# Attention and a Fourier filter layer on one core: loads of k and v as 96 x 6 rows, a shared filter fold, and a reordered last batch

## The chip, the cores and the metric

The kernel runs on one core of one Trainium2 chip. Times are device microseconds of one execution. The number to predict is the median over such executions, which for the kernel before is 233.95 us. TensorE (PE in the profile) does matmuls, VectorE (DVE) and ScalarE (ACT) elementwise work, GpSimd (POOL) elementwise work and the loads that change the type, SyncE (SP) issues other DMAs.

## The reference

There are 8 batches, 8 heads, 576 positions, 64 elements per head; the model width is 512.

```python
def _attn_ref(q, k, v, g_norm):
    kv = np.einsum('bhsd,bhse->bhde', k, v)
    out = np.einsum('bhsd,bhde->bhse', q, kv)
    rms = np.sqrt(np.mean(out * out, axis=-1, keepdims=True) + 1e-06)
    return out / rms * g_norm

def _moe_ref(x, w_proj, filter_fft, w_out):          # x: heads side by side, (8, 576, 512)
    proj = x @ w_proj
    x1, x2, x3 = ...                                 # thirds of proj
    X2 = np.fft.rfft(x2, axis=1)
    H = np.fft.rfft(filter_fft, axis=0)[None]
    x2_conv = np.fft.irfft(X2 * H, axis=1)
    y = x1 * x2_conv * x3
    return y @ w_out
```

## The kernel before, in words

All matmuls are in bf16. `load_kv` and `load_q` bring k, v and q of a batch to SBUF through GpSimd's DMA queue, which turns fp32 into bf16 on the way. k and v lie as 128 partitions by 4 rows of the sequence, which covers 512 of 576 rows; the other 64 rows are a load of their own (`kvt`, L75). Buffers are double: batch b uses set b % 2. All loads of the start (q, k, v of batch 0, three parts of `w_proj`, the filter twice, q, k, v of batch 1, `w_out`) are on that one queue in this order. The filter comes once straight (`fa`, three rows to a partition, L150) and once mirrored through an indirect DMA with an index tile (`fc`, L153); both load 112 rows (NL) of which 97 are used.

For a batch, `kv` (L247) multiplies k by v in five chunks of the sequence and copies the 64 x 64 blocks into a block-diagonal tile `kvblk`; `qtr` transposes q; `att_o` multiplies the two, squares the result on ScalarE (L298) and scales it by g_norm on VectorE or ScalarE (L300 to L303); `att_r` sums the squares over a head with a matmul and takes the reciprocal root on ScalarE; `att_x` multiplies to x, and `fold` (VectorE) builds sums and differences of x over thirds and mirror images, so that the Fourier transform of length 576 becomes matmuls of 97 and 128 rows. `proj2` projects the folded x to x2, `fft(b, g)` transforms it in three groups g (two VectorE products per group for the complex product with the filter's spectrum HH, their sum on Pool at L426 or on VectorE at L428; group 2 is one product with HM, L433) into Y. `proj13` makes x1 (ScalarE copy) and the gate g13 = x1 * x3 (VectorE, L450); `inv` is the inverse transform with its unfolding on VectorE, and `outp` multiplies by `w_out` and stores.

The filter's own spectrum is made once: `filter_angles` and `filter_tables` compute its sines and cosines FH on VectorE and ScalarE, `tables` transposes the inverse's tables IV on TensorE and copies them to FW and FX on VectorE, `fold_filter` (L347) adds and subtracts `fa` and `fc` into `ff` (two VectorE operations), `gen_h(g)` multiplies FH by ff (L364, L368), and ScalarE scales the result to HH and HM.

The main program is L609 to L698. Ahead of the loop, TensorE gets filler matmuls (`warm`), then batch 0's attention in two halves (two head pairs each). Each pass of the loop over b runs the filter layer of batch b interleaved with the attention of batch b + 1 and the output of batch b - 1. Pass b = 0 has an order of its own that holds the filter's spectrum. The last batch ends in `last` (L537): an inverse split so that the first and last row blocks are done first, then the output of batch 6 and five pieces of output (`out1`).

The program is written in this order, but a scheduler orders each engine's instructions by when it believes their inputs to be ready, with program order as the priority, and inserts the waits. `tc.keep_in_program_order(ins)` pins an instruction behind everything written before it for its engine. PSUM is one pool of four tiles (`psp`), each two banks; a matmul group waits for a free one. GpSimd's and SyncE's DMAs have a limited number in flight: a further one waits for an older one to land.

Of the kernel before, what the change touches and what calls it, by code (L numbers as in the profile page):

```python
# [15 lines left out]
P = 128  # L16
# [4 lines left out]
def kernel(  # L21
# [39 lines left out]

    NR = S // 64
    kvm = [[consts.tile([P, H, 4, D], BF16, name="%sm%d" % (n, i)) for n in "kv"] for i in range(2)]
# [3 lines left out]
    def load_kv(b, *parts):  # L67
        for h0, h1 in parts:
            for i, src in enumerate((k, v)):
                nc.gpsimd.dma_start(  # L70
                    out=kvm[b % 2][i][:, h0:h1].rearrange("p h c d -> p h (c d)"),
                    in_=bass.AP(tensor=src.tensor, offset=src.offset + (b * H + h0) * S * D,
                                ap=[[4 * D, P], [S * D, h1 - h0], [1, 4 * D]]))
                if h0 == 0:
                    nc.gpsimd.dma_start(out=kvt[b % 2][i][:TAIL], in_=src[b, :, 4 * P:S, :].transpose([1, 0, 2]))  # L75
# [73 lines left out]
    NL = 112  # L149
# [70 lines left out]
    FX = consts.tile([P, 4, P], BF16)  # L220

    def tables():
        nc.vector.memset(FX[0:96, 0], 0.0)
        d0, d1 = (psp.tile([P, 2, 8, P], BF16, name="ps_ft", tag="ps")[:, 0] for _ in range(2))
        lo, hi = slice(0, 64), slice(64, P)
        tr, cp = nc.tensor.transpose, nc.vector.tensor_copy
        for i in range(2, 6):
            tr(d0[:, i], IV[:, i, 0:P], ident)
        tr(d0[0:96, 0], IV[:, 0, 0:96], ident)
        tr(d0[96:P, 6], IV[:, 1, 0:32], ident)  # L230
        for r in (lo, hi):
            tr(d0[r, 7], IV[:, 1, 32:96], ident)
        for i in range(2, 6):
            tr(d1[lo, i], IV[:, i, P:SB], ident)
        for i in (3, 5):
            tr(d1[hi, 6 + i // 5], IV[:, i, P:SB], ident)
        cp(out=FW[:, 0, 2:6], in_=d0[:, 2:6])
        cp(out=FW[lo, 1, 2:6], in_=d1[lo, 2:6])
        cp(out=FX[hi, 2:4], in_=d1[hi, 6:8])
        cp(out=FW[0:96, 0, 0], in_=d0[0:96, 0])  # L240
        cp(out=FX[96:P, 0], in_=d0[96:P, 6])
        cp(out=FX[:, 1], in_=d0[:, 7])
# [4 lines left out]
    def kv(b, j0=0, j1=NDC):  # L247
        (km, vm), (kt, vt) = kvm[b % 2], kvt[b % 2]
        kvp = ps_tile("ps_kv")
        for j in range(j0, j1):  # L250
            for c in range(NSC):
                for hp in range(2):
                    h = 2 * j + hp
                    kk, vv = (km[:, h, c], vm[:, h, c]) if c < 4 else (kt[:, h], vt[:, h])
                    mm = nc.tensor.matmul(kvp[64 * hp:64 * hp + 64, 0, j * D:(j + 1) * D], kk, vv,  # L255
                                          start=(c == 0), stop=(c == NSC - 1))
                    if b == 1:
                        tc.keep_in_program_order(mm)
        for h in range(2):
            r = slice(64 * h, 64 * h + 64)  # L260
            o_ = kvblk[b % 2][r, j0:j1, r]
            i_ = kvp[r, 0, j0 * D:j1 * D].rearrange("p (j e) -> p j e", e=D)
            if b == 0 and j0 == 0:
                nc.vector.tensor_copy(out=o_, in_=i_)
            else:
                nc.scalar.copy(out=o_, in_=i_)  # L266
# [23 lines left out]
    def att_o(b, j):  # L290
# [9 lines left out]
        if b == 0 or b == 1 and j != 2:  # L300
            nc.vector.tensor_scalar_mul(out=o_, in0=op[:, :, 0:TH], scalar1=g_col)
        else:
            nc.scalar.activation(out=o_, in_=op[:, :, 0:TH], func=AF.Copy, scale=g_col)  # L303
# [43 lines left out]
    def fold_filter():  # L347
        ff = hst['ff'] = work.tile([P, 2, 3, DM], BF16, name="ff", tag="ff")
        for i, op in enumerate((nc.vector.tensor_add, nc.vector.tensor_sub)):
            tc.keep_in_program_order(op(out=ff[:N1, i], in0=fa[:N1], in1=fc[:N1]))  # L350
# [52 lines left out]
    def fft(b, g):  # L403
# [7 lines left out]
        if g < 2:  # L411
# [13 lines left out]
            if g or b in (0, B - 1):  # L425
# [111 lines left out]
    def last(b):  # L537
# [21 lines left out]
        proj13(b, NDC - 1)  # L559
# [30 lines left out]
        for c in (0, 2):  # L590
            outp(b - 1, c)
# [21 lines left out]
    for jj in range(2):  # L613
# [8 lines left out]
        fold(0, jj)  # L622
    filter_tables()
    tables()
    for b in range(B):
# [7 lines left out]
        if b == 0:  # L633
# [6 lines left out]
            gen_h(2)  # L640
            qtr(1, (0,))
            fft(0, 0)
            qtr(1, (1,))
            fft(0, 2)
            kv(1)
# [8 lines left out]
        if b == 0:  # L654
# [3 lines left out]
            att_r(1, 1)  # L658
            proj13(0, 2)
            att_x(1, 0)  # L660
            fold(1, 0)
            att_o(1, 2)
# [7 lines left out]
        for dc in range(NDC if nxt else NDC - 1) if b else ():  # L670
            if dc < 3:
                add = (fft(b, (1, 0, 2)[dc]) if dc or not nxt else None) or (dc and add)
            if nxt and dc == 0:
# [3 lines left out]
            else:  # L677
                if nxt:
                    att_o(b + 1, dc)
# [3 lines left out]
            if nxt:  # L683
                att_r(b + 1, dc)
                if dc % 2:
                    att_x(b + 1, dc // 2)
                    fold(b + 1, dc // 2)
            if b and nxt and dc in (1,):
                outp(b - 1, 2 * (1,).index(dc))
        if not nxt:  # L690
            last(b)
# [37 lines left out]
```

## Time and profile before

| what | us |
|---|---|
| median of 14 runs | 233.95 |
| lowest and highest | 232.27 and 235.31 |
| the profiled execution, its own time | 234.17 |
| its span, first to last instruction | 232.1 |
| TensorE busy | 210.2 |
| VectorE busy | 193.7 |
| ScalarE busy | 157.8 |
| Pool busy | 73.0 |
| mean granted TensorE clock | 0.986 |

All times within the profile count from the start of the span. In a line of the timeline the first number is the start, the second the busy time of the group; then come engine, line, operation, output <- inputs, shape and count, and in brackets how long the engine stood idle before and what released it. In the chain of work the two numbers are start and duration. The row by slices cuts the span into 40 parts of 5.8 us; a digit is the busy share in tenths. Releasers are inferred from semaphores, so a named one can be the last of several.

### The profile page before, as it was taken

Reading aid. Unit: us, or ns where it says so; the run is one execution under the profiler, and the core shown is the slowest. Engines: PE = TensorE matmul, PEld = TensorE weight load, DVE = VectorE, ACT = ScalarE, POOL = GpSimd, SP = SyncE. Lnnn points to the kernel's source line nnn. Section 1 sums busy time; section 2 is a strip of 40 time slices with the busy share of each in tenths; the row PEclk is TensorE's granted clock in tenths of the full one; section 3 lists DMA queues with packets and bytes.
Section 4 is the critical chain, followed back from the end, with each engine's and each line's share of the span. In section 5 each row is a group of like instructions: output and inputs, shape, how many; then the busy total and the mean of one; then the engine's idle time right before and its main releaser. Section 6 shows DMA issues by size and latency. Waiting matters only on the chain.

```text
span 232.1 us, 4858 instructions
## 1 busy us (share of the span) xinstructions
PE 210.2 (91%) x1941; PEld 128.4 (55%) x1967; DVE 193.7 (83%) x369; ACT 157.8 (68%) x230; POOL 73.0 (31%) x87
## 2 busy tenths in 40 slices
PE   4967789779999999999999999999999999999970
PEld 1434265464657565755766576656675666566520
DVE  6967776898997998798897989797979897997940
ACT  2738946875869597958975897769776977533340
POOL 7983363960650056003800380004000300016010
PEclk9979999999999999999999999999999999999997
DMA  5999999999897349932991299150033003500086
GB/s 63 149 174 227 240 192 199 190 191 189 97 187 133 93 45 183 172 80 67 174 214 25 71 162 205 34 134 1 12 82 90 3 0 93 136 0 3 0 214 193
DMA packets 45543, 27.37 MB, mean 118 GB/s; under 512 B 22242, under 2 KB 40674, under 8 KB 45522
## 3 DMA queue, kind: packets, MB, share of 16 engines
q0 software_dynamic: 40240, 17.90, 60.4%
q1 hardware_dynamic: 5042, 8.78, 14.4%
q10 hardware_dynamic: 240, 0.39, 0.6%
q8 instruction: 15, 0.25, 0.4%
q14 instruction: 6, 0.05, 0.1%
HBM read 33.88 MB, written 9.44 MB: 187 GB/s over the span
## 4 chain that ended last, share of the span: by engine, by line
PE 75%; POOL 8%; DMA 6%; DVE 3%; issue 3%; ACT 2%; POOLq 0%; DVEq 0%
PE ps_x L444 23%; PE ps_out L506 10%; DMA fc<-in_moe_filter_fft_dram,fidx 6%; PE ps_x L393 5%; PE ps_qT L279 3%; PE ps_o L297 3%; PE ps_r L312 3%; PE ps_x L384 3%; PE ps_x L399 3%; PE ps_invo L470 2%; POOL Y L426 2%; PE ps_kv L255 2%; PE ps_inve L470 2%; PE ps_x L387 2%; PE ps_out L528 2%
## 5 line engine op out<-in xcount | busy, mean ns | idle before, releaser
L444 PE MATMUL ps_x<-x,wp 128*128 128x288 bf16 x512 | 69.0, 286 | 0.0
L444 PEld LDWEIGHTS <-wp 128*128 128x128 bf16 x512 | 49.2, 98 | 14.3 <-issue 0.9
L426 POOL TENSOR_TENSOR Y<-tpw 128x1024 bf16<-128x1024 f32 (+1 forms) x10 | 23.5, 2353 | 70.3 <-DVE tpw L424 70.3
L450 DVE TENSOR_TENSOR g<-ps_x,x 128x576 bf16<-128x576 f32 x32 | 24.0, 753 | 10.9 <-ACT x L448 7.5
L70 POOL DMA_DIRECT2D km<-in_k_dram x9 | 8.0, 885 | 61.7 <-PE ps_kv L255 58.2
L313 ACT ACTIVATE rstd<-ps_r,bias_eps 128x576 bf16<-128x576 f32 x32 | 23.3, 743 | 5.5 <-PE ps_r L312 5.5
L506 PE MATMUL ps_out<-wo,yg 128*128 128x512 bf16 x99 | 25.6, 379 | 0.7
L448 ACT CAST x<-ps_x 128x576 bf16<-128x576 f32 x32 | 20.5, 641 | 8.1 <-PE ps_x L444 8.1
L514 ACT COPY ot<-ps_out 128x1024 f32<-128x1024 f32 (+1 forms) x17 | 15.9, 937 | 14.6 <-PE ps_out L506 14.6
L298 ACT ACTIVATE sq<-ps_o 128x576 bf16<-128x576 f32 x32 | 20.5, 650 | 6.3 <-PE ps_o L297 5.6
L423 DVE TENSOR_TENSOR tpw<-ps_X,HH 128x1024 f32<-128x1024 f32 (+1 forms) x16 | 19.5, 1222 | 3.4 <-PE ps_X L421 1.7
L424 DVE TENSOR_TENSOR tpw<-ps_X,HH 128x1024 f32<-128x1024 f32 (+1 forms) x16 | 19.4, 1213 | 0.0
L303 ACT ACTIVATE osb<-ps_o,g_col 128x576 bf16<-128x576 f32 x25 | 18.5, 739 | 0.0
L393 PE MATMUL ps_x<-wp,ab 128*128 128x512 bf16 x61 | 15.5, 381 | 1.6 <-DVE ab L339 1.3
L506 PEld LDWEIGHTS <-yg 128*128 128x128 bf16 x112 | 11.0, 98 | 10.8
L474 ACT COPY os<-ps_invo 128x576 f32<-128x576 f32 x14 | 9.0, 640 | 10.5 <-PE ps_x L387 5.1
L288 ACT COPY qT<-ps_qT 128x1152 bf16<-128x1152 bf16 x14 | 15.6, 1119 | 0.7
L297 PE MATMUL ps_o<-qT,kvblk 128*128 128x288 bf16 x64 | 13.0, 297 | 2.7 <-ACT kvblk L266 1.5
L312 PE MATMUL ps_r<-sq,ind 128*128 128x288 bf16 x64 | 13.4, 295 | 2.2 <-ACT sq L298 1.8
L606 PE MATMUL ps_w<-kvblk,ind 128*128 128x512 bf16 x31 | 10.3, 481 | 3.9 <-DVE ind L103 3.4
L321 DVE TENSOR_TENSOR x<-osb,rstd 128x1152 bf16<-128x1152 bf16 x16 | 12.1, 754 | 1.7 <-ACT rstd L313 1.7
L79 POOL DMA_DIRECT2D qb<-in_q_dram x16 | 12.6, 791 | 1.4 <-POOLq L713 0.8
(210 smaller groups left out, 405.7 us busy)
## 6 DMA issues: line engine op xcount, KB each, us to landing
out_dram<-ot SPq DMA_DIRECT2D x28, 256.0 KB, 3.3
qb<-in_q_dram POOLq DMA_DIRECT2D x16, 288.0 KB, 6.4
km<-in_k_dram POOLq DMA_DIRECT2D x7, 512.0 KB, 6.4
vm<-in_v_dram POOLq DMA_DIRECT2D x7, 512.0 KB, 8.1
wp<-in_moe_w_proj_dram POOLq DMA_DIRECT2D x3, 512.0 KB, 12.0
out_dram<-ot SPq DMA_DIRECT2D x6, 128.0 KB, 3.3
fa<-in_moe_filter_fft_dram POOLq DMA_DIRECT2D x1, 672.0 KB, 15.4
km<-in_k_dram POOLq DMA_DIRECT2D x2, 256.0 KB, 4.2
```

The costliest lines, as they stand in the source:

```text
L297: nc.tensor.matmul(op[:, h, 0:TH], kvblk[b % 2][:, j], s['qT'][:, 2 * (j % 2) + j // 2, h * TH:(h + 1) * TH], start=True, stop=True)
L298: nc.scalar.activation(out=s['sq'][:, j].rearrange("p (a b) -> p a b", a=2), in_=op[:, :, 0:TH], func=AF.Square)
L312: nc.tensor.matmul(r2[:, h, 0:TH], ind, s['sq'][:, j, h * TH:(h + 1) * TH], start=True, stop=True)
L313: nc.scalar.activation(out=s['rstd'][:, j].rearrange("p (a b) -> p a b", a=2), in_=r2[:, :, 0:TH], func=AF.Abs_reciprocal_sqrt, scale=1.0 ...
L393: nc.tensor.matmul(pp[:, h], ab[:, j, h * SB:h * SB + P], wp[:, j, DM:2 * DM], start=(j == 0), stop=(j == NDC - 1))
L423: nc.vector.tensor_mul(out=t_[:n, 0], in0=xp[:n], in1=HH[:n, g, 1:3])
L424: nc.vector.tensor_mul(out=t_[:n, 1], in0=xp[:n], in1=HH[:n, g, 0:2])
L426: nc.gpsimd.tensor_add(out=Y[:n, 2 * g:2 * g + 2], in0=t_[:n, :, 0], in1=t_[:n, :, 1])
L444: nc.tensor.matmul(pp[:, h, 0:TH], w_, x[:, j, h * TH:(h + 1) * TH], start=(j == 0), stop=(j == NDC - 1))
L448: nc.scalar.copy(out=x1, in_=pp[:, :, 0:TH])
L450: nc.vector.tensor_mul(out=st[b]['g13'][:, dc].rearrange("p (a b) -> p a b", a=2), in0=pp[:, :, 0:TH], in1=st[b]['x1', dc])
L506: nc.tensor.matmul(pp[:, cc], yg[:, dc, c * P:(c + 1) * P], wo[:, dc], start=(dc == 0), stop=(dc == NDC - 1))
```

## The change

- k and v of batches 0 and 1 are loaded as 96 partitions by 6 rows, which covers all 576 rows, so their tail loads are gone. Their `kv` runs six chunks of 96 rows in place of five. Later batches are as before, in wider tiles.
- The filter is loaded 96 rows at a time; the 97th, one row of 512, comes through SyncE's queue into each of `fa` and `fc`.
- `fold_filter` becomes six operations: Pool takes the third of the three filter rows of each partition (both the sum and the difference), VectorE the other two, all pinned.
- `tables` comes ahead of `filter_tables`, its copies are pinned, and a clearing of FX moves to the start. The first copy into `kvblk` of batch 0 moves from VectorE to ScalarE, as does the scale of batch 0's last head pair.
- In pass 0, kv(1) comes ahead of gen_h(2) and fft(0, 2); att_x(1, 0) and att_o(1, 2) come ahead of proj13(0, 2).
- In the last batch, both remaining transforms come ahead of proj13(7, 1); of group 0's sum Pool makes half and VectorE the other; half the output of batch 6 comes ahead of the inverse, and proj13(7, 2) behind the inverse's matmuls.

```diff
@@ -59,19 +59,21 @@
 
 
 
     NR = S // 64
-    kvm = [[consts.tile([P, H, 4, D], BF16, name="%sm%d" % (n, i)) for n in "kv"] for i in range(2)]
+    kvm = [[consts.tile([P, H, 6, D], BF16, name="%sm%d" % (n, i)) for n in "kv"] for i in range(2)]
     kvt = [[consts.tile([P, H, D], BF16, name="%st%d" % (n, i)) for n in "kv"] for i in range(2)]
     qb = [consts.tile([P, 4, NR * D], BF16, name="qb%d" % i) for i in range(2)]
 
     def load_kv(b, *parts):
+        n, C = (96, 6) if b < 2 else (P, 4)
         for h0, h1 in parts:
             for i, src in enumerate((k, v)):
                 nc.gpsimd.dma_start(
-                    out=kvm[b % 2][i][:, h0:h1].rearrange("p h c d -> p h (c d)"),
+                    out=kvm[b % 2][i][:n, h0:h1, 0:C].rearrange("p h c d -> p h (c d)"),
                     in_=bass.AP(tensor=src.tensor, offset=src.offset + (b * H + h0) * S * D,
-                                ap=[[4 * D, P], [S * D, h1 - h0], [1, 4 * D]]))
-                if h0 == 0:
+                                ap=[[C * D, n], [S * D, h1 - h0], [1, C * D]]))
+                if h0 == 0 and b > 1:
                     nc.gpsimd.dma_start(out=kvt[b % 2][i][:TAIL], in_=src[b, :, 4 * P:S, :].transpose([1, 0, 2]))
 
     def load_q(b):
@@ -146,7 +148,9 @@
     nc.gpsimd.iota(fidx, pattern=[[-1, 3]], base=S, channel_multiplier=-3)
     nc.gpsimd.memset(fidx[0:1, 0:1], 0)
 
-    NL = 112
+    NL = N1 - 1
+    for t in (fa, fc):
+        nc.sync.dma_start(out=t[NL:N1, 0], in_=moe_filter_fft[TH:TH + 1])
     nc.gpsimd.dma_start(out=fa[:NL], in_=bass.AP(
         tensor=moe_filter_fft.tensor, offset=moe_filter_fft.offset, ap=[[3 * DM, NL], [1, 3 * DM]]))
     for a in range(3):
@@ -218,12 +222,12 @@
 
     FW = consts.tile([P, 2, 6, P], BF16)
     FX = consts.tile([P, 4, P], BF16)
+    nc.vector.memset(FX[0:96, 0], 0.0)
 
     def tables():
-        nc.vector.memset(FX[0:96, 0], 0.0)
         d0, d1 = (psp.tile([P, 2, 8, P], BF16, name="ps_ft", tag="ps")[:, 0] for _ in range(2))
         lo, hi = slice(0, 64), slice(64, P)
-        tr, cp = nc.tensor.transpose, nc.vector.tensor_copy
+        tr, cp = nc.tensor.transpose, lambda **kw: tc.keep_in_program_order(nc.vector.tensor_copy(**kw))
         for i in range(2, 6):
             tr(d0[:, i], IV[:, i, 0:P], ident)
         tr(d0[0:96, 0], IV[:, 0, 0:96], ident)
@@ -248,22 +252,20 @@
         (km, vm), (kt, vt) = kvm[b % 2], kvt[b % 2]
         kvp = ps_tile("ps_kv")
         for j in range(j0, j1):
-            for c in range(NSC):
+            n, nc_ = (96, 6) if b < 2 else (P, NSC)
+            for c in range(nc_):
                 for hp in range(2):
                     h = 2 * j + hp
-                    kk, vv = (km[:, h, c], vm[:, h, c]) if c < 4 else (kt[:, h], vt[:, h])
+                    kk, vv = (km[:n, h, c], vm[:n, h, c]) if b < 2 or c < 4 else (kt[:, h], vt[:, h])
                     mm = nc.tensor.matmul(kvp[64 * hp:64 * hp + 64, 0, j * D:(j + 1) * D], kk, vv,
-                                          start=(c == 0), stop=(c == NSC - 1))
+                                          start=(c == 0), stop=(c == nc_ - 1))
                     if b == 1:
                         tc.keep_in_program_order(mm)
         for h in range(2):
             r = slice(64 * h, 64 * h + 64)
             o_ = kvblk[b % 2][r, j0:j1, r]
             i_ = kvp[r, 0, j0 * D:j1 * D].rearrange("p (j e) -> p j e", e=D)
-            if b == 0 and j0 == 0:
-                nc.vector.tensor_copy(out=o_, in_=i_)
-            else:
-                nc.scalar.copy(out=o_, in_=i_)
+            nc.scalar.copy(out=o_, in_=i_)
 
     def qtr(b, jjs=(0, 1)):
 
@@ -297,7 +299,7 @@
             nc.tensor.matmul(op[:, h, 0:TH], kvblk[b % 2][:, j], s['qT'][:, 2 * (j % 2) + j // 2, h * TH:(h + 1) * TH], start=True, stop=True)
         nc.scalar.activation(out=s['sq'][:, j].rearrange("p (a b) -> p a b", a=2), in_=op[:, :, 0:TH], func=AF.Square)
         o_ = s['o'][:, j].rearrange("p (a b) -> p a b", a=2)
-        if b == 0 or b == 1 and j != 2:
+        if b == 0 and j < 3 or b == 1 and j != 2:
             nc.vector.tensor_scalar_mul(out=o_, in0=op[:, :, 0:TH], scalar1=g_col)
         else:
             nc.scalar.activation(out=o_, in_=op[:, :, 0:TH], func=AF.Copy, scale=g_col)
@@ -346,8 +348,9 @@
 
     def fold_filter():
         ff = hst['ff'] = work.tile([P, 2, 3, DM], BF16, name="ff", tag="ff")
-        for i, op in enumerate((nc.vector.tensor_add, nc.vector.tensor_sub)):
-            tc.keep_in_program_order(op(out=ff[:N1, i], in0=fa[:N1], in1=fc[:N1]))
+        for eng, n, s_ in ((nc.gpsimd, N1 - 1, slice(2, 3)), (nc.vector, N1, slice(0, 1)), (nc.vector, N1 - 1, slice(1, 2))):
+            for i, op in enumerate((eng.tensor_add, eng.tensor_sub)):
+                tc.keep_in_program_order(op(out=ff[:n, i, s_], in0=fa[:n, s_], in1=fc[:n, s_]))
 
     def gen_h(g):
 
@@ -422,7 +425,10 @@
             t_ = work.tile([P, 2, 2, DM], FP32, name="tpw", tag="tpw", bufs=2)
             nc.vector.tensor_mul(out=t_[:n, 0], in0=xp[:n], in1=HH[:n, g, 1:3])
             nc.vector.tensor_mul(out=t_[:n, 1], in0=xp[:n], in1=HH[:n, g, 0:2])
-            if g or b in (0, B - 1):
+            if g == 0 and b == B - 1:
+                nc.gpsimd.tensor_add(out=Y[:n, 1], in0=t_[:n, 1, 0], in1=t_[:n, 1, 1])
+                return lambda: nc.vector.tensor_add(out=Y[:n, 0], in0=t_[:n, 0, 0], in1=t_[:n, 0, 1])
+            if g or b == 0:
                 nc.gpsimd.tensor_add(out=Y[:n, 2 * g:2 * g + 2], in0=t_[:n, :, 0], in1=t_[:n, :, 1])
                 return
             return lambda: nc.vector.tensor_add(out=Y[:n, 2 * g:2 * g + 2], in0=t_[:n, :, 0], in1=t_[:n, :, 1])
@@ -556,7 +562,8 @@
                 for g in (1, 2):
                     nc.tensor.matmul(pb[:, h, dc * 64:(dc + 1) * 64], Y[:, 2 * g + h, dc * P:(dc + 1) * P],
                                      IV[:, 2 * g + h, P:SB], start=(g == 1), stop=(g == 2))
-        proj13(b, NDC - 1)
+        for dc in (2, 3):
+            proj13(b, dc)
         osa = work.tile([P, 2, 2 * M], FP32, name="osa", tag="tpw", bufs=2)
         osb_ = work.tile([P, NDC * 64], FP32, name="osb_", tag="os")
         nc.scalar.copy(out=osa, in_=tiles[1][:, :, 0:2 * M])
@@ -587,8 +594,7 @@
         dv.tensor_add(out=w[:, :, 64:S].rearrange("p j (x c) -> p j x c", c=2 * P)[:, :, :, 64:P], in0=ub, in1=rr_)
         mid = slice(P, 7 * 64)
         dv.tensor_mul(out=yg[:, :, mid], in0=w[:, :, mid], in1=g13[:, :, mid])
-        for c in (0, 2):
-            outp(b - 1, c)
+        outp(b - 1, 2)
         act, dve = nc.scalar.copy, nc.vector.tensor_copy
         q0, q1, q2 = nc.sync, nc.scalar, nc.gpsimd
         ot = lambda tag, bufs: work.tile([P, 4, DM] if tag == "tpw" else [P, 2, DM] if tag == "ot" else [P, 3, DM],
@@ -620,8 +626,8 @@
         warm(3)
         att_x(0, jj)
         fold(0, jj)
+    tables()
     filter_tables()
-    tables()
     for b in range(B):
         nxt = b + 1 < B
         proj2(b)
@@ -637,12 +643,12 @@
             gen_h(1)
             gen_h(0)
             fft(0, 1)
-            gen_h(2)
             qtr(1, (0,))
             fft(0, 0)
             qtr(1, (1,))
+            kv(1)
+            gen_h(2)
             fft(0, 2)
-            kv(1)
         elif nxt:
             kv(b + 1)
             qtr(b + 1, (0,))
@@ -656,10 +662,10 @@
             att_o(1, 1)
             att_r(1, 0)
             att_r(1, 1)
+            att_x(1, 0)
+            att_o(1, 2)
             proj13(0, 2)
-            att_x(1, 0)
             fold(1, 0)
-            att_o(1, 2)
             att_o(1, 3)
             att_r(1, 2)
             att_r(1, 3)
@@ -667,27 +673,32 @@
             fold(1, 1)
             proj13(0, 3)
             fins = [inv(0, (0, 1))]
-        for dc in range(NDC if nxt else NDC - 1) if b else ():
+        for dc in range(NDC) if b and nxt else ():
             if dc < 3:
-                add = (fft(b, (1, 0, 2)[dc]) if dc or not nxt else None) or (dc and add)
-            if nxt and dc == 0:
+                add = (fft(b, (1, 0, 2)[dc]) if dc else None) or (dc and add)
+            if dc == 0:
                 proj13(b, 0, (0,))
                 att_o(b + 1, 0)
                 proj13(b, 0, (2,))
             else:
-                if nxt:
-                    att_o(b + 1, dc)
+                att_o(b + 1, dc)
                 proj13(b, dc)
             if dc == 2 and add:
                 add()
-            if nxt:
-                att_r(b + 1, dc)
-                if dc % 2:
-                    att_x(b + 1, dc // 2)
-                    fold(b + 1, dc // 2)
-            if b and nxt and dc in (1,):
-                outp(b - 1, 2 * (1,).index(dc))
+            att_r(b + 1, dc)
+            if dc % 2:
+                att_x(b + 1, dc // 2)
+                fold(b + 1, dc // 2)
+            if dc == 1:
+                outp(b - 1, 0)
         if not nxt:
+            for dc, g in enumerate((1, 0)):
+                add = fft(b, g)
+                if dc:
+                    fft(b, 2)
+                    add()
+                proj13(b, dc)
+            outp(b - 1, 0)
             last(b)
             continue
         if b:
```

## The prediction

> **What bounds the kernel now.** I read the page first. TensorE is busy for 91% of the span, and the row by slices shows where it isn't: slices 1 to 9 (one is 5.8 us) and the last.
>
> ```profile
> PE 210.2 (91%) x1941; PEld 128.4 (55%) x1967; DVE 193.7 (83%) x369; ACT 157.8 (68%) x230; POOL 73.0 (31%) x87
> ...
> PE   4967789779999999999999999999999999999970
> ```
>
> From 54 us to 212 us TensorE hardly stops, and the change leaves those batches alone. What it touches is the first 54 us, where TensorE waits, and the last 20. So I next read the chain of work that ended last, between 16 and 34 us:
>
> ```profile
> 16.55 13.68 DMA fc<-in_moe_filter_fft_dram,fidx
> 30.23 0.03 issue
> 30.25 0.05 DVEq L350
> 30.30 0.04 issue
> 30.35 0.92 DVE ff L350
> 31.27 0.75 issue
> 32.02 1.76 DVE ff L350
> 33.79 0.05 issue
> 33.83 2.78 PE ps_h L364 x12
> ```
>
> The gathered filter `fc` lands at 30.23 us, VectorE folds for 3.4 us, then TensorE starts the spectrum `ps_h`. One chain is not a bound, so I asked the timeline what TensorE and VectorE did meanwhile (start, busy us, engine, line):
>
> ```profile
> 12.34 0.32 PE L255 MATMUL ps_kv<-vm,km 128*64 128x64 bf16 x8 [0.62 <-DMA vm<-in_v_dram]
> ...
> 23.11 0.42 DVE L237 COPY FW<-ps_ft 128x512 bf16<-128x512 bf16 x1 [0.61 <-PE ps_ft L232]
> 23.45 0.75 DVE L321 TENSOR_TENSOR x<-osb,rstd 128x1152 bf16<-128x1152 bf16 x1
> ...
> 33.83 0.39 PE L364 MATMUL ps_h<-ff,FH 97*128 97x512 bf16 x1 [0.66 <-DVE ff L350]
> ```
>
> TensorE waited only 0.66 us for the fold: a second chain (k, v of batch 0, attention, `x`, fold of `x`, proj2, proj13) is just behind. Landing the filter sooner alone is worth 0.66 us; both chains must move. The second has a stall of its own: `x` at 23.45, although its `rstd` was done at 22.22, because a table copy (L237) stood before it on VectorE, waiting for TensorE.
>
> At the end I read the timeline and SyncE's waits:
>
> ```profile
> 213.13 0.22 PE L553 MATMUL ps_invo<-IV,Y 97*128 97x96 bf16 x1 [0.40 <-POOL Y L426]
> ...
> 222.04 0.57 PEld L531 LDWEIGHTS <-yg 128*64 128x64 bf16 x8 [0.53 <-DVE yg L589]
> ...
> 228.68 0.47 SPq L534 DMA_DIRECT2D out_dram<-ot__3310  x1
> ```
> ```profile
> SPq L534 <- DMA out_dram<-ot__3288: 0.9, 1, 0.9
> ```
>
> The last result is in SBUF at 225.73 us (L532), but its second half is issued at 228.68, after an earlier store has landed. The stretches from 221 to 230 us show a DMA share of 0.68 to 1.07: the end is a queue of stores.
>
> **What the Trainium skill says.** "DMA: Bandwidth & Descriptors", section "Why a DMA increments its semaphore by 16 and not by 1": a load of 96 partitions spreads over 16 engines, an odd count over few. That speaks for 96 rows plus a single row; no run here shows 97. The same page, "Specifications", asks for at least 512 B per transfer. The trace agrees in part: the tail of k in batch 0 (128 B writes, 131 KB read) took 1.36 us between landings (9.14 to 10.5), in batch 1 only 0.45. "GPSIMD Engine Reference", section 3.1: a two-input op is about twice as slow as on VectorE. The trace agrees: L426 on Pool 2.36 us, the same add on VectorE (L428) 1.21. Its section 1 says that Pool's SBUF interface is shared with VectorE instructions of two SBUF inputs; the trace has no such pair that tells a price.
>
> **Part 1, the loads.** A landing is the issue plus the time to landing. q of batch 0 is in at 7.7, its k and v at 16.05: 8.35 us for 2.36 MB. 1.96 of that are the two tails; the four halves (0.524 MB read) took 1.45 to 1.7. With 96 x 6 rows the tails are gone and a part reads 0.590 MB. At the slowest of the halves (1.7) it would take 1.9, at batch 1's rate (1.05 MB in 2.5 us) 1.4; I take 1.55, so 6.2 instead of 8.35: 2.15 sooner (0.75 to 2.75; a loss is excluded, fewer packets with the same bytes). The filter took from 24.9 (last `wp` landing) to 30.23; 96 of 112 rows save a seventh of 5.33 us, 0.76. `fc` then lands at 27.3. Two row loads go to SyncE's queue, which holds only `g_col` then: nothing. Pool issues two fewer DMAs per batch at 0.7 us, which are ahead of `wp`; issue is not what bounds, since the queue is some 5 us deep by then.
>
> **Part 2, the chain of x.** The warm-up matmuls end at 11.72, so kv can start at 11.75 instead of 12.34 and, without the wait for the tail at 12.77, ends at 12.45 with its 24 matmuls (20 before). The copy on ScalarE, idle here, costs 0.63 from kv to `ps_o` (18.62 to 19.25 in the second half) against 1.22 now: `ps_o` at 13.1, not 14.37. From there to the end of `rstd` it is 3.88 us now at a TensorE clock of 0.50 to 0.69 (14 to 18 us), 2.97 in the second half at full clock; I take a mean gain, 1.6 for the second kv. `rstd` of the second half then ends at 20.7 instead of 22.22; the scale of head pair 3, moved to ScalarE (0.73, ahead of `rstd`), makes it 21.45. `x` starts there, not at 23.45, as the table copies are pinned behind the fold; `x` and fold take 2.6 instead of 2.95 (one copy less): 24.1 against 26.40. From the fold's end TensorE needs 6.7 us for proj2, proj13(0,0) and (0,1) (26.46 to 33.16), whose weights land before 23. So `ps_h` starts at 30.85 instead of 33.83: **3.0 sooner**. The copies now lie after the fold: 1.8 us, to 25.9, beside proj2; its third PSUM tile needs them at 25.8. That is the cover, and it is thin: 0.1 to 0.3 if it fails.
>
> **The filter's fold.** VectorE now does two thirds: a 97x1536 op is 1.755, so about 0.62 for 512, four make 2.5; Pool two of 512 at half of 2.36, 2.4. From 27.3 both end at 29.8, 1.0 before TensorE is ready. If they take turns at SBUF the sum is 4.9: 32.2, so 1.4 of the gain lost. I take no cost and keep that end. Pool's two ops stand in its queue; behind them are the loads of batch 2, which have 8 us to spare.
>
> **Part 3, batch 1's attention.** kv(1) goes before gen_h(2), so `ps_o` no longer waits 0.85 for the copy on ScalarE and gen_h(2) fills that gap; 8 matmuls more cost 0.16 (40 take 0.78). VectorE is nearly full from 37.4 to 53.15 with about 1.7 idle, of which an earlier att_o(1,2) can win a part. From both sides: +0.3 to -1.2; I take **-0.4**. k and v of batch 1 land at 27.3 + 2.8 (q) + 2 x 2.75 = 35.6; kv(1), pinned, is due at 36.8: 1.2 to spare.
>
> **Part 4, the end.** TensorE's work is only reordered. Of Pool's 2.36 us add, half moves to VectorE (0.7), and the 0.40 and 0.04 that TensorE waits at 213 go. But proj13(7,2) behind the inverse puts its gate multiply (0.75) into VectorE's last row of work, full from 214.84 to 221.99; this starts 0.65 sooner (inverse at 212.0, no stop). So L531 is where it was, 222.05: zero, -0.4 to +0.7. Stores: 0.52 MB (outp(6,0)) leave the queue of 2.36 MB for a time when DMA is idle (212 to 220). At the 240 GB/s of 222 to 228 us that is 2.2 us of transfer; since the last stores wait also for their results and issue, I take half: **-1.1**, 0 to -2.2.
>
> **Sum:** -3.0 - 0.4 - 1.1 = -4.5. The profiled execution took 234.17 us (span 232.1, 2.07 around it), 0.22 over the median of 233.95. So 229.45, say 229.5.
>
> **Rivals.**
> - *Bytes bind, not packets.* For: batch 1's tails took only 0.45. Then only the filter's seventh is gained: `fc` at 29.5, folded at 32.0, `ps_h` at 32.1 (-1.7); with -0.3 and -0.5 for the rest that is -2.5: 231.4. The same time comes out if Pool and VectorE take turns. Against: 8.35 us in batch 0.
> - *All of it, at full clock.* If the shorter idle time before 14 us keeps the clock up, x gains 0.5 more; with -1.2 in batch 1 and -1.8 at the end: -6.5, 227.4.
> - *Pool becomes the bound of the fold* (the slower side). Before, Pool issued batch 2's loads between 30.75 and 37.2, ahead of work that the program has before them, and each waited for an older load to land (vt for km: 1.6). If the fold is ordered behind all these, its last issue waits for batch 1's k (32.9), so Pool folds from 33.7 to 36.1, and `ps_h` starts at 36.2: +2.4, less the end's 1.1: +1.3, 235.2. It decides for slower once Pool's fold ends after about 35.6. Against: its ops are pinned behind wo's load and come first in the program.
> - *It nets to nothing:* the fold half as late, or kv(1) waiting, with no gain at the end: 233.7.
>
> **Numbers.** Forecast 0.56 (228.3 to 230.7 of its own), bytes bind 0.16, full gain 0.12, Pool 0.10, nothing 0.06. 0.3%, 0.7 us, is about what a measurement here can tell from no change. Faster 0.84, same 0.06, slower 0.10. The range takes in the two faster rivals with most of their width, 226.8 to 232.4, and leaves out Pool and nothing.
>
> **What would show it.** `fc` landing near 27.3 (if 29.5, bytes bind); ps_kv from 11.75; `x` of the second half before 22; `ps_h` from 30.9, waiting for proj13 rather than `ff`; Pool's `ff` between 27 and 30, ahead of batch 2's km (behind it, the slower rival); ps_o of batch 1 8.6 after `ps_h` (9.0 now); no wait for Pool at the last inverse; L531 at the same distance from batch 7's start; the last store issued within 2 us of L532's last copy (2.95 now). The forecast is wrong if TensorE waits anew before 54 us, on kv(1) or on PSUM.

## The result, and the profile after

| | before | after |
|---|---|---|
| median, us | 233.94 (47 runs, 232.27 to 235.59) | 231.14 (10 runs, 230.24 to 232.39) |
| profiled execution: time, span | 234.17, 232.1 | 231.05, 229.3 |
| TensorE, VectorE busy in it | 210.2, 193.7 | 209.6, 194.8 |

The ratio after to before is 0.9884, with a 95% interval of 0.9864 to 0.9903: 2.8 us faster, where 4.5 was forecast. The sign and the range held, and the end went as described. The start gained much less than forecast, and one of its steps, the filter's fold at no cost, failed. The forecast's own range (228.3 to 230.7) was missed by 0.4, and the time is nearer the 231.4 of the rival "bytes bind". That it is not further off is in part luck: the end gave more than forecast, where the start gave less.

The page of after shows the start less empty, and the end in one slice:

```profile
PE 209.6 (91%) x1956; PEld 128.0 (56%) x1983; DVE 194.8 (85%) x369; ACT 158.2 (69%) x233; POOL 71.4 (31%) x85
...
PE   4868879889899999999999999999999999999990
```

Both chains of the prediction have moved. The gathered filter releases Pool's fold at 28.86 us (before, the fold of VectorE at 30.23), and proj13's last matmuls give way to `ps_h` at 31.39 (before 33.83). But the chain of work of after shows what became of these 2.4 us (start, duration):

```profile
27.86 1.79 DVE ff L353 x3
29.66 1.10 issue
30.76 0.85 DVE ff L353
31.61 0.82 issue
32.43 0.75 DVE g L456
33.19 0.04 issue
33.23 0.59 PE ps_h L367 x2
...
35.59 2.03 ACT HH L375 x2
```

ScalarE makes the first HH at 35.59. Before, it was 35.35. So at this point **nothing is left** of what both chains had gained, although TensorE's clock from 14 to 18 us was full in this execution and 0.55 and 0.60 in the one of before. The timeline says why (start, busy us, engine, line; in brackets what the engine waited for):

```profile
28.86 3.11 POOL L353 TENSOR_TENSOR ff<-fa,fc 96x512 bf16<-96x512 f32 x2 [1.74 <-DMA fc<-in_moe_filter_fft_dram,fidx]
29.07 3.44 DVE L353 TENSOR_TENSOR ff<-fa,fc 96x512 bf16<-96x512 f32 x2
...
31.39 0.38 PE L367 MATMUL ps_h<-ff,FH 97*128 97x512 bf16 x1
...
32.56 0.38 PE L367 MATMUL ps_h<-ff,FH 96*128 96x512 bf16 x1 [0.79 <-DVE ff L353]
...
33.23 0.59 PE L367 MATMUL ps_h<-ff,FH 97*97 97x512 bf16 x2 [0.29 <-DVE g L456]
...
33.66 0.38 PE L422 MATMUL ps_X<-x,FW 128*128 128x512 bf16 x1
...
34.51 1.91 PE L367 MATMUL ps_h<-ff,FH 96*128 96x512 bf16 x8
...
35.59 1.02 ACT L375 ACTIVATE HH<-ps_h 128x1024 f32<-128x1024 f32 x1 [4.34 <-PE ps_h L367]
```

Two things are to be seen. VectorE's last two operations of the fold take 3.44 us side by side with Pool's. And TensorE runs four spectrum matmuls, then the four of batch 0's first transform (L422 to L424), and only then the other eight; before, the twelve stood in a row. HH, which the transform's product needs in any case, waits for the first part's matmuls in that last group.

What the start gains in these two traces appears only later: `ps_o` of batch 1 starts at 41.67 (before 42.85), and batch 2's kv at 56.56 (57.84), so 1.28 us. From there to the end the trace gives another 1.52, taken up below.

### The profile page after: what moved, and what is told of

Its sections match the earlier page's. It is cut to its first block, busy times and chain, and to the rows that moved or that the text cites. A ratio compares the mean times of both kernels' runs of the same rounds, so it can differ in the third digit from the quotient of the medians.

```text
span 229.3 us, 4892 instructions
## 1 busy us (share of the span) xinstructions
PE 209.6 (91%) x1956; PEld 128.0 (56%) x1983; DVE 194.8 (85%) x369; ACT 158.2 (69%) x233; POOL 71.4 (31%) x85
## 4 chain that ended last, share of the span: by engine, by line
PE 73%; DVE 7%; DMA 6%; POOL 4%; ACT 4%; issue 3%; POOLq 0%; DVEq 0%
PE ps_x L450 24%; PE ps_out L512 9%; DMA fc<-in_moe_filter_fft_dram,fidx 6%; PE ps_x L396 6%; PE ps_o L299 3%; PE ps_r L314 3%; PE ps_qT L281 3%; PE ps_x L387 3%; PE ps_x L402 3%; PE ps_invo L476 2%; PE ps_inve L476 2%; PE ps_x L390 2%; PE ps_kv L260 2%; PE ps_out L534 2%; PE ps_X L419 1%
## 5 line engine op out<-in xcount | busy, mean ns | idle before, releaser
L432 POOL TENSOR_TENSOR Y<-tpw 128x1024 bf16<-128x1024 f32 (+1 forms) x9 | 21.2, 2358 | 71.0 <-DVE tpw L427 71.0
L426 DVE TENSOR_TENSOR tpw<-ps_X,HH 128x1024 f32<-128x1024 f32 (+1 forms) x16 | 19.5, 1222 | 3.2 <-PE ps_X L419 1.6
L305 ACT ACTIVATE osb<-ps_o,g_col 128x576 bf16<-128x576 f32 x26 | 19.2, 739 | 0.0
L612 PE MATMUL ps_w<-kvblk,ind 128*128 128x512 bf16 x31 | 9.6, 454 | 3.8 <-DVE ind L105 3.4
```

What stands on the lines that cost most here:

```text
L426: nc.vector.tensor_mul(out=t_[:n, 0], in0=xp[:n], in1=HH[:n, g, 1:3])
L432: nc.gpsimd.tensor_add(out=Y[:n, 2 * g:2 * g + 2], in0=t_[:n, :, 0], in1=t_[:n, :, 1])
```

## The experiments

Every kernel was run six to 22 times, and timed against the kernel before on the same chip, whose medians were 234.13, 233.95 and 234.06 us on the three chips used. The last six rows are the kernel with the whole fold on VectorE with one more thing changed.

| kernel | median, us | ratio, 95% interval |
|---|---|---|
| before with the last batch's edits alone | 232.32 | 0.9924, 0.9891 to 0.9957 |
| after, last batch as before | 233.09 | 0.9954, 0.9933 to 0.9976 |
| after, whole fold on VectorE | 229.32; again 230.01 | 0.9797, 0.9758 to 0.9835; 0.9823, 0.9791 to 0.9856 |
| after, first kvblk copy on VectorE | 231.23 | 0.9875, 0.9837 to 0.9913 |
| after, spectrum matmuls pinned | 229.90 | 0.9855, 0.9820 to 0.9889 |
| whole fold on VectorE, with k and v as before | 231.05 | 0.9863, 0.9830 to 0.9897 |
| whole fold on VectorE, filter rows as before | 230.78 | 0.9851, 0.9817 to 0.9885 |
| whole fold on VectorE, differences ahead of sums | 230.25 | 0.9835, 0.9799 to 0.9870 |
| whole fold on VectorE, half of the output of batch 6 back | 232.93 | 0.9948, 0.9928 to 0.9969 |
| whole fold on VectorE, table copies as before | 229.97 | 0.9828, 0.9781 to 0.9875 |
| whole fold on VectorE, FX cleared later | 228.89 | 0.9798, 0.9767 to 0.9828 |

### The two ends apart

The last batch's hunks of the diff alone on the kernel before, and all of the diff but these.

> The kernel before with only the edits of the last batch. Reading the two traces, the start is worth 1.3 us (kv of batch 2 starts at 56.56 instead of 57.84) and the end 1.5. If so: 232.4 us, the last store issued about 3 us sooner relative to the start of batch 7 than before. If the end's part was only 1.1 as predicted: 232.8. If the stores hide nothing and all of the gain is from the start: 233.9.

> The changed kernel with the last batch as before. The complement of the run above: 232.6 us if the start is worth 1.3 and the two parts add up; 230.5 if the start had its predicted 3.4; 231.2 if the end is worth nothing.

Measured: 232.32 and 233.09, so 1.8 for the end and 1.0 for the start. They add up to 2.8, which is what the whole change brings: as far as intervals of some 0.8 and 0.5 us to each side can tell, the parts do not get in each other's way. The gap to the forecast lies in the start (3.4 forecast, 1.0 measured); the end gave 0.7 more than its 1.1. The trace of the second run, with the start of after at a clock of 0.50 to 0.97 from 14 to 20 us, has batch 2's kv at 57.05, not at 56.56. So a part of the 1.28 above is likely the fuller clock.

### The fold on VectorE alone

```diff
-for eng, n, s_ in ((nc.gpsimd, N1 - 1, slice(2, 3)), (nc.vector, N1, slice(0, 1)), (nc.vector, N1 - 1, slice(1, 2))):
+for eng, n, s_ in ((nc.vector, N1, slice(0, 1)), (nc.vector, N1 - 1, slice(1, 2)), (nc.vector, N1 - 1, slice(2, 3))):
```

> The changed kernel with all six fold operations on VectorE. Theory: Pool and VectorE take turns at SBUF (VectorE's four took 4.65 us where four times 0.62 were expected), and the planner, which expects Pool's third late, puts the spectrum's matmuls apart. Then each VectorE operation takes 0.69, the fold is over at 31.2 or before instead of 32.4, all twelve ps_h matmuls run in a row, the first HH is scaled some 2 us sooner, and the time is 229.5 to 230.5. Rival: the filter's landing (28.8 instead of the predicted 27.3) is what cost; then six operations in a row end at 31.5 or later and the time is 231.1 or more.

> The same kernel as the one with all six operations of the filter's fold on VectorE, run again beside three variants of it, so that they are compared on one chip. Expected 229.3 (229.0 to 229.8). In its trace the fold's six operations take 3.7 us on VectorE, from about 28.9 to 32.6, and the spectrum's matmuls follow in a row of twelve.

Measured: 229.32 and, on another chip, 230.01; after is 231.14. So **taking Pool's share away is worth 1.1 to 1.8 us**, with both intervals clear of after's, and the kernel without it is where the prediction's 229.5 was. The fold is not over by 31.2, as the theory had it, but at 32.6 and 31.7. It need not be: the spectrum's matmuls start at 33.39 and 31.09, behind proj13. VectorE's groups by shape show the price of the sharing (busy us, mean ns of one; after, then the second of these runs):

```profile
L353 DVE TENSOR_TENSOR ff<-fa,fc 96x512 bf16<-96x512 f32 x2 | 3.4, 1755 | 0.0
...
L353 DVE TENSOR_TENSOR ff<-fa,fc 97x512 bf16<-97x512 f32 x2 | 1.3, 688 | 0.7 <-issue 0.7
```
```profile
L353 DVE TENSOR_TENSOR ff<-fa,fc 96x512 bf16<-96x512 f32 x4 | 2.5, 681 | 0.0
```

An operation that takes 0.68 us takes 1.755 while Pool folds. On VectorE alone six take 3.70 us; shared, VectorE takes 4.65 for four.

### Price of the sharing, or the order it brought?

The kernel with the whole fold on VectorE differs from after in a second thing: its twelve spectrum matmuls are in a row again. This run keeps the shared fold and pins the matmuls.

```diff
-nc.tensor.matmul(hp[:n, i], FH[:m, a, 1 - i, f0:f0 + n], ff[:m, 1 - i, a], **kw)
+tc.keep_in_program_order(nc.tensor.matmul(hp[:n, i], FH[:m, a, 1 - i, f0:f0 + n], ff[:m, 1 - i, a], **kw))
```

> The changed kernel, its fold shared with Pool as it is, but the twelve spectrum matmuls of the first two parts held in the order of the program, so that they come in a row again, ahead of the four of batch 0's first transform. Theory 'the loss of 1.4 lies in the two engines slowing each other at SBUF': the fold still ends near 32.4 and the twelve end some 2.8 after that or a little sooner; the time falls by no more than 0.5: 230.6 to 231.2. Rival 'it lies in the order of TensorE that the shared fold brought with it': the time falls to that of the kernel with the whole fold on VectorE, 229.3 to 230.0.

Measured: a median of 229.90, 1.2 below after; the intervals of the ratios overlap a little, so the medians alone do not prove it. The two traces can be compared, for TensorE's clock is full throughout the start in both. The timeline of this run:

```profile
31.16 0.38 PE L367 MATMUL ps_h<-ff,FH 97*128 97x512 bf16 x1
...
32.35 2.55 PE L367 MATMUL ps_h<-ff,FH 96*128 96x512 bf16 x11 [0.80 <-DVE ff L353]
...
33.63 1.02 ACT L375 ACTIVATE HH<-ps_h 128x1024 f32<-128x1024 f32 x1 [2.61 <-PE ps_h L367]
```

VectorE's fold is as slow as in after (4.64 us for four), and TensorE still waits 0.80 for it, yet HH is made 1.96 us sooner, and `ps_o` of batch 1 starts at 40.47 instead of 41.67. In the kernel with the whole fold on VectorE it starts at 40.10. Proj13 begins at 27.46, 27.23 and 27.16 in the three. So of the distance from after, about 1.0 at `ps_o` is TensorE's order and 0.3 what is left of the slow fold: the rival is right for most of it.

That the slow fold costs only 0.3 here has a reason of its own. In that trace of the kernel with the whole fold on VectorE, kv(1) waits 0.48 for v of batch 1, taken up below. In the first run of the same kernel it does not wait:

```profile
29.46 4.09 PE L450 MATMUL ps_x<-x,wp 128*128 128x288 bf16 x32
...
38.78 0.93 PE L260 MATMUL ps_kv<-vm,km 96*64 96x64 bf16 x48
...
41.68 0.69 PE L299 MATMUL ps_o<-qT,kvblk 128*128 128x288 bf16 x4
```

`ps_o` comes 12.22 us after proj13, where it is 13.24 with the shared fold and pinned matmuls, and 14.21 in after. So the slow fold and the changed order cost about 1.0 each, and v takes back most of the first where it lands late.

The two programs differ in nothing but the engine of the fold, so it was the shared fold that brought the other order here. It does not always: the kernel with the first kvblk copy on VectorE, next section, shares the fold too, and its transform waits until the twelve are done.

```profile
33.25 0.60 PE L370 MATMUL ps_h<-ff,FH 97*128 97x512 bf16 x2
34.05 2.33 PE L370 MATMUL ps_h<-ff,FH 97*97 97x512 bf16 x10 [0.21 <-DVE g L459]
```

On what grounds the scheduler chooses was not tried.

### Where the chain of x lost time

Prediction: with the copy on ScalarE, idle here, `ps_o` at 13.1. It starts at 14.51. The timeline of after:

```profile
11.19 0.35 DVE L181 TENSOR_TENSOR ang<-ang 128x192 f32<-128x192 f32 x1
...
12.16 0.57 PE L260 MATMUL ps_kv<-vm,km 96*64 96x64 bf16 x24
...
12.63 1.28 ACT L186 ACT_TABLE_LOAD   x1
...
13.93 0.53 ACT L268 CAST kvblk<-ps_kv 64x128 bf16<-64x128 f32 x2
...
14.51 0.67 PE L299 MATMUL ps_o<-qT,kvblk 128*128 128x288 bf16 x4 [1.78 <-ACT kvblk L268]
```

ScalarE is not idle: VectorE finishes the third angle at 11.5, behind the two copies of q (before: 9.4, ahead of both), so ScalarE's sines and table load end at 13.9 (before 11.8). Two runs on this: the copy back on VectorE, and FX cleared later in the program, after which VectorE has the old order of angle and q.

```diff
-            nc.scalar.copy(out=o_, in_=i_)
+            if b == 0 and j0 == 0:
+                nc.vector.tensor_copy(out=o_, in_=i_)
+            else:
+                nc.scalar.copy(out=o_, in_=i_)
```
```diff
-    nc.vector.memset(FX[0:96, 0], 0.0)

     def tables():
...
     qtr(0)
+    nc.vector.memset(FX[0:96, 0], 0.0)
```

> The changed kernel with the first copy into kvblk back on VectorE. The copy on ScalarE stood behind a table load until 13.93 us, 1.2 after kv was done. If that is on the path that sets the end: ps_o of batch 0 at 13.4 instead of 14.51 and up to 1 us off, 230.2. If the fold and the spectrum bound the start, as the theory has it: ps_o sooner, the time within 0.3 of 231.14.

> The kernel with the whole fold on VectorE, and the clearing of FX placed in the program after the transposes of q instead of ahead of the tables. VectorE then finishes the third angle before it copies q, and the table copies stay behind the fold of x. ScalarE's copy of the first kv block no longer stands behind a late sine and the table load: about 1.3 sooner by the profile (13.6 to 12.3). Theory 'the chain of x still sets the start': the first attention matmuls begin near 13.2 and the time falls by 0.5 to 1.2: 229.0. Rival 'the filter and v of batch 1 bind now': no change, 229.5 to 230.0.

Measured: 231.23 for the first (after: 231.14), no gain. The second half of the copy now waits on VectorE behind L203 (the halves start at 13.73 and 15.00), and `ps_o` starts at 15.36, not at the 13.4 that was expected. But this kernel also has the twelve matmuls in a row, which was worth about 1.0 above, so the equal time does not tell what the later `ps_o` costs. The second, on top of the whole fold on VectorE, has the lowest median of all, 228.89, and is the best version found; but its interval overlaps that of the kernel it is built on. In its trace ScalarE is free from 12.2 us and the copy's wait is put down to TensorE's kv; `ps_o` comes 1.68 after kv instead of 2.13. q landed late in this execution, so kv itself is at 12.67 (12.07), `ps_o` at 14.35 where 13.2 was expected, and the trace as a whole shows no gain. It is of this kernel's slowest execution (229.60), and does not show where the lower median comes from. The reading that the clearing of FX moved the angle behind q rests on the order of instructions in the two programs, which differ in its place alone; that it costs the 0.4 or 1.1 us between the medians is not shown.

### The loads, the fold's order and the tables, one by one

Four kernels with the whole fold on VectorE, each with one part undone or changed.

```diff
-        n, C = (96, 6) if b < 2 else (P, 4)
+        n, C = P, 4
```

> The kernel with the whole fold on VectorE, but k and v of batches 0 and 1 again as 128 partitions by 4 rows plus the two tails. Theory 'the 96-partition layout is what starts the chain sooner': v of batch 0 lands about 0.9 later, the filter behind it 0.9 later as well, and the time rises by 0.9 to 1.3: about 230.4. Rival 'the start's gain comes from the other edits (table copies pinned behind the fold, kv of batch 1 ahead of the last spectrum part, the copies' engines)': the time stays within 0.4 of it: 229.3 to 229.7, although the landings move.

Measured: 231.05 beside 230.01, so 1.0 as the first theory has it, though the intervals of the two overlap. Last half of v of batch 0 at 16.1 instead of 15.2, last gather at 29.2 instead of 28.7. Its trace, from its fastest execution (229.83), shows only 0.5 at x and 0.2 at batch 2's kv, so the rest of that 1.0 has no place in a trace.

```diff
-    NL = N1 - 1
-    for t in (fa, fc):
-        nc.sync.dma_start(out=t[NL:N1, 0], in_=moe_filter_fft[TH:TH + 1])
+    NL = 112
```

> The kernel with the whole fold on VectorE, but the filter again loaded and gathered as 112 rows instead of 96 and a single row. A seventh more bytes in the four transfers. Theory 'the filter's landing sets the fold, and the fold the spectrum's start': the last gather lands 0.5 to 0.8 later and the time rises by about 0.5: 229.8. Rival 'the fold is not what TensorE waits for': no change, 229.3. Should an odd count of rows matter rather than bytes, the landings would not move at all, since both counts are even multiples of 16: then 229.3 too.

Measured: 230.78 beside 230.01, so 0.8; again the intervals overlap. The last gather lands at 29.5 instead of 28.7, as a seventh more bytes would have it. VectorE waits 0.86 for `fc`.

Its trace shows one thing more. This is the only changed start without the two single-row loads on SyncE's queue, and q's second half lands at 7.8, as in both kernels with the start as before (7.8 and 7.9). In the eleven traces with these loads it lands between 8.5 and 9.4, the one with k and v as before among them (8.8). So the row loads, which come first on SyncE's queue, go with q landing about 1 us later. How they do it, and what it costs in the end, is open; v of batch 0 lands no later for it (15.2 in after, 15.4 without them).

```diff
-        for eng, n, s_ in ((nc.vector, N1, slice(0, 1)), (nc.vector, N1 - 1, slice(1, 2)), (nc.vector, N1 - 1, slice(2, 3))):
-            for i, op in enumerate((eng.tensor_add, eng.tensor_sub)):
+        for i, op in ((1, nc.vector.tensor_sub), (0, nc.vector.tensor_add)):
+            for n, s_ in ((N1, slice(0, 1)), (N1 - 1, slice(1, 2)), (N1 - 1, slice(2, 3))):
```

> The kernel with the whole fold on VectorE, but its three differences ahead of its three sums (before: sum and difference of each slice in turn). The first six of the twelve spectrum matmuls read only differences in their first three and only sums in the next three. Theory 'in this kernel the fold is again the last thing that the spectrum waits for': the first matmuls can start some 0.7 us sooner, and the time falls by 0.3 to 0.7: 228.8. Rival 'TensorE comes from proj13 no sooner than the fold ends': no change, 229.3. The last gather lands just ahead of the fold, so that the three differences wait for it together: if that costs, it is slower by up to 0.5: 229.8.

Measured: 230.25 beside 230.01, no change: `ps_h` follows proj13 at 31.72 in its trace, and by then the fold is over (27.60 and 3.70 for six, 31.3). The rival holds.

```diff
-        tr, cp = nc.tensor.transpose, lambda **kw: tc.keep_in_program_order(nc.vector.tensor_copy(**kw))
+        tr, cp = nc.tensor.transpose, nc.vector.tensor_copy
...
-    tables()
     filter_tables()
+    tables()
```

> The kernel with the whole fold on VectorE, but its table copies where they were before: not held in program order, the clearing of FX inside them, called after the filter's tables. One of them then stands again ahead of the second half of x on VectorE. With it comes an order of VectorE in which the third angle is finished ahead of the copies of q, as it was before the change. Theory 'x of the second half gains what its stall of 1.2 was': the time rises by 0.5 to 1.0: 230.4. Rival 'the landing of the filter and of v of batch 1 bind now, so a later x is hidden': 229.5 to 229.9. If the third angle's earlier end is worth more than the stall, it falls: 229.2.

Measured: 229.97 (228.42 to 231.24, and one execution of 232.96) beside 230.01 and 228.89. With the angle's old order and the table copies not pinned, the stall on x is back (23.01 instead of 21.87 in the run with FX cleared later, of which 0.6 is that run's earlier start of the attention), and the medians of these two lie 1.1 apart, with overlapping intervals. The medians would fit that the pinned copies gain about what their stall was, and that the late angle that came with them takes most of it away. The trace does not show the second half: the angle is early, but the first copy into kvblk starts only at 14.34, some 1.2 us after kv has ended, and what held it is not known. So how the two share is open.

### What holds the start now

The chain of work in the second run with the whole fold on VectorE no longer goes through the filter:

```profile
24.09 13.13 DMA vm<-in_v_dram
37.23 0.14 issue
37.36 0.95 PE ps_kv L260 x48
```

v of batch 1 is issued at 24.09, when an older load has landed, and lands at 37.23; kv(1), pinned, waits for it (0.48). In the run with half of the output back, whose start is the same, v lands at 36.9, and kv(1) starts at 37.09 without a wait: there the chain goes through x, proj13 and the twelve spectrum matmuls. So v of batch 1 and the chain of x are level.

### What the end's gain is made of

```diff
-            outp(b - 1, 0)
             last(b)
...
-        outp(b - 1, 2)
+        for c in (0, 2):
+            outp(b - 1, c)
```

> The kernel with the whole fold on VectorE, with half of the output of batch 6 moved back behind the inverse of the last batch, the other edits of the end kept. Theory 'the stores that leave the last queue are what the end gains': it loses most of 1.8 again: 231.0 to 231.5. Rival 'the end gains by the halved addition on Pool and the inverse that starts sooner': it loses no more than 0.5: 229.6 to 230.2.

Measured: 232.93, so 3.3 lost against the mean of 229.32 and 230.01, more than the first theory asked for (231.0 to 231.5); 2.4 of it is in the trace. A line of its timeline, then SyncE's last three issues of stores in it, and those of after:

```profile
208.59 0.23 PE L557 MATMUL ps_invo<-IV,Y 128*128 128x128 bf16 x1 [0.92 <-DVE Y L439]
```
```profile
222.74 1.77 SPq L540 DMA_DIRECT2D out_dram<-ot__3307  x1
...
224.60 1.05 SPq L540 DMA_DIRECT2D out_dram<-ot__3320  x1
226.32 0.47 SPq L540 DMA_DIRECT2D out_dram<-ot__3329  x1
```
```profile
222.40 1.23 SPq L540 DMA_DIRECT2D out_dram<-ot__3307  x1
...
223.72 0.85 SPq L540 DMA_DIRECT2D out_dram<-ot__3320  x1
...
224.67 0.85 SPq L540 DMA_DIRECT2D out_dram<-ot__3329  x1
```

The last batch can be measured free of the start: from batch 2's kv to the 64-row block of the output (L531 before, L537 after), and from there to the span's end.

| kernel | kv(2) at | to the 64-row block | to the end |
|---|---|---|---|
| before | 57.84 | 164.20 | 10.06 |
| after, last batch as before | 57.05 | 164.21 | 10.04 |
| before with the last batch's edits | 57.31 | 163.90 | 8.89 |
| after | 56.56 | 163.92 | 8.82 |
| whole fold on VectorE (second run) | 54.66 | 163.94 | 8.80 |
| whole fold on VectorE, half of the output back | 54.58 | 165.00 | 10.12 |

The columns repeat within 0.04 and 0.09 where the code is the same. The edits of the end are worth 0.28 up to the 64-row block and 1.24 behind it, and the moved output is needed for both. Without it the stores' tail is back (+1.32), with the last issue 3.06 behind the last copy (2.95 before, 0.51 in after). And TensorE has nothing to fill the 0.92 and 0.16 that it then waits for VectorE, and does the eight matmuls (1.7) in its last row of work instead: +1.06.

## Why the prediction was right, and where it was not

- **Loads, -2.15 for k and v, -0.76 for the filter.** Sizes off. v of batch 0 landed at 15.2 (forecast 13.9, before 16.05): 0.85. `fc` came 1.4 sooner, not 2.9. The rate of k and v's parts is the term. In the run with 112 filter rows, where q was in at 7.8 as before, v landed at 15.4: 7.6 us for four parts of 0.590 MB, so 1.9 a part, where 1.55 was taken and 1.9 stood as the slow end. The filter's rows were right (0.8 at the last gather in the run with 112). The two row loads on SyncE's queue were put at nothing, and q lands about 1 us later with them. The rule for odd counts that the prediction takes from the Trainium skill has, in the same section, an exception for some copies on GpSimd's queue; no run loads 97 rows, so none shows which holds here.
- **Chain of x, -3.0.** It came to 2.44 (33.83 to 31.39). `ps_o` failed by 1.4. The step "the copy on ScalarE, idle here" was read from before's trace, in which the third angle was done at 9.4; the change moved it. kv itself started at 12.16 and not at 11.75, with q's transposes later too (8.95, before 8.47). The full clock that this execution had from 14 to 18 us gave part of it back; the prediction had taken a mean between that and the clock of before. x of the second half started at 22.03 (forecast 21.45), released by `rstd`, no longer by a table copy: this step was right.
- **The filter's fold, no cost.** This is the step that failed. The prediction had named, and not taken, what came: "If they take turns at SBUF the sum is 4.9: 32.2, so 1.4 of the gain lost". VectorE's four operations took 4.65 us where 2.5 was put, and the fold ended at 32.5. The Trainium skill says it more sharply than the page that the prediction used: "SBUF — State Buffer", section "SBUF: two separate sides", has the pair of ports shared by VectorE and GpSimd as an exclusive lock, held for a whole instruction, against VectorE operations with two SBUF inputs. The trace agrees in the main: 1.755 instead of 0.68 us, 1.07 more, where a Pool operation of this size takes 1.27 alone; from Pool's start the two engines need 3.65 us for what is 3.9 one after the other. The 1.4 was close in size, but its path was not foreseen: at `ps_o` the slow fold costs about 1.0 by itself, of which v's landing leaves 0.3, and the changed order of TensorE, which the prediction did not consider, costs another 1.0.
- **Batch 1, -0.4.** Undersized. From HH to `ps_o` it takes 6.08 instead of 7.50: -1.4, and this is what the start gained in the end. But only about half of it is a gain of its own, because HH was late and other work went ahead of it: from `ps_h`, `ps_o` comes 10.28 later in after, 9.02 before, and 8.29 in the first run with the whole fold on VectorE (8.6 forecast), so 0.7. Where HH comes 2.8 sooner (32.83, the second such run), the stretch takes 7.27, as kv(1) waits for v. The forecast had v of batch 1 at 35.6, with 1.2 to spare; it lands at 37.2, with nothing to spare.
- **The end, -1.1 and zero.** Right in mechanism: -1.24 behind the 64-row block, where the stores are, and -0.28 up to it. "TensorE's work is only reordered" left out that the moved matmuls also cover VectorE's part of Y; that is what the run without them showed.
- **The rivals.** "Bytes bind" gave nearly the right time (231.4), but not by its path: `fc` at 28.8 lies between its 29.5 and the forecast's 27.3. Pool as the bound did not happen: its fold ran from 28.86 to 32.0, ahead of batch 2's loads.

## What to carry to other kernels

Before work is shared between VectorE and Pool, look at whether both read two SBUF inputs, as here: if they do, price the sum of both, not the longer one, and read the order of the instructions that follow, for it may change too and cost more. A wait that is removed at one place is worth only the distance to the next thing that is late; here the filter, x and v of the next batch came within 1 us of each other. An "idle" engine in the trace before is idle in that order of instructions; a moved clearing of a table was enough to fill it.

## What was not expected of the hardware

- VectorE and Pool on one tile: 0.68 to 1.755 us for 96 x 512 on VectorE, 1.27 to 1.43 and 1.71 on Pool (after; 1.266 and 1.269 in the run where VectorE began 1.4 us later than Pool). Not every pair does this. In the trace of before, VectorE's product of a PSUM and an SBUF tile (L423, L424) takes 1.21 to 1.23 us beside Pool's addition (L426), and 1.21 without it; Pool takes 2.35 or 2.36 every time.
- The granted TensorE clock at the start differs between executions: 0.55 and 0.60 from 14 to 18 us in the one of before, 0.60, 0.50, 0.50 and 0.70 from 16 to 24 us in the first run with the whole fold on VectorE, 1.00 throughout in the second. Between these last two, executions of one kernel, `ps_h` moved by 2.30 us (33.39, 31.09), of which 0.62 was there at the first kv (12.69, 12.07), and `ps_o` of batch 1 by 1.58 (41.68, 40.10). The Trainium skill, "TensorE: Matmul & The Clock Gate", Part 1, has a gate that follows how busy TensorE has been lately; it is busy in pieces there, and why one execution is granted less than another is not shown. So two single traces of the start can be compared only where their clocks are alike, and otherwise the medians decide.
- 96 rows land in proportion to their bytes: with 112 rows the last of the four transfers landed 0.8 us later (one trace each), where the prediction had worked out 0.76.
